# Last 128 output rows: from two halves copied by ScalarE and VectorE to three pieces copied by ScalarE alone

## The chip, the cores and the metric

The kernel runs on one core of a Trainium2 chip. The metric is the device time of one execution in microseconds, here the median over several runs. A core has engines with instruction queues of their own: TensorE (matmuls; its weight loads are listed apart), VectorE, ScalarE, GpSimd, and SyncE, which issues DMAs. ScalarE and GpSimd can issue DMAs too. TensorE writes its results to PSUM; VectorE and ScalarE copy them to SBUF, and a DMA carries them from there to HBM.

## The reference

A causal attention with a sliding window of 64, on 8 batches, 8 heads, 576 positions and 64 dimensions per head, followed by a gated feed-forward layer on the 4608 tokens of 512 values:

```
scores = scale * q @ k.T                 # per batch and head
mask   = (rel >= 0) & (rel < 64)         # rel = query position - key position
attn   = softmax(where(mask, scores, -1e9))
x      = (attn @ v)  as [4608, 512]      # heads side by side
out    = (maximum(x @ w_gate, 0) * (x @ w_val)) @ w_out    # d_ff = 1536
```

Inputs and output are float32; the output has 4608 rows of 512 columns.

## The kernel before

The tokens are cut into four tiles of 384 and six tiles of 512 (`starts`, `widths`). For each tile, attention makes `xt`, the transposed input of the feed-forward layer, in fp16. `hidden(t)` then multiplies it with slices of `w_gate` and `w_val` (L468), ScalarE takes the relu (L453), and VectorE multiplies both halves into `g_sb`, which holds the 12 slices (`NF`) of d_ff with the tile's tokens (L456). `output(t)` multiplies `g_sb` with `w_out`: for each block of 128 rows, 12 matmuls of 512 columns accumulate in one PSUM bank (L482, in `out_mm`), where the slice of `g_sb` is the stationary operand, so that each matmul has its own weight load of 128x128. `out_evac` copies the bank to SBUF on ScalarE (L489) and SyncE issues the store (L490).

The order is written by hand in a manual schedule: TensorE's feed-forward work is emitted in program order, and a planner (`Weaver`) with an estimated clock emits copies and the attention of the next tile at due times between the matmuls. At the end of the last tile its heap is empty (`W.drain()`), and everything comes out in program order.

The last tile ends in `output_last`. Its first three row blocks go through `output`. The last 128 rows are made in two halves of 256 columns, each with 12 matmuls (L514) into a PSUM tile of its own. The first half is copied by ScalarE and stored over SyncE's queue; the second half is copied in two quarters, one by ScalarE, stored over ScalarE's own queue, one by VectorE, stored over SyncE's queue (L520, L521).

Two rotations matter. The PSUM tiles come from `f_ps` (L84): four banks under one tag that `op_tile` and the `h` tiles of `hidden` share. The SBUF tiles `o_sb` come from `f_sb` (L83): three buffers, so that a fourth `o_sb` must wait until the store of the first has landed. The pool `consts` (L76) has one buffer for each name and is never rotated. At the end of the program (L699) the queues wait for all stores and for each other.

Of the kernel before, what the change touches and what calls it, by code (L numbers as in the profile page):

```python
# [10 lines left out]
FP32 = mybir.dt.float32  # L11
# [33 lines left out]
def kernel(  # L45
# [10 lines left out]
    nc = tc.nc  # L56
    B, H, S, D = q.shape
    DM = H * D
# [14 lines left out]
    starts = [TT * t for t in range(NS)] + [NS * TT + WT * t for t in range(NL)]  # L73
    widths = [TT] * NS + [WT] * NL

    consts = ctx.enter_context(tc.tile_pool(name="consts", bufs=1))  # L76
# [6 lines left out]
    f_sb = ctx.enter_context(tc.tile_pool(name="f_sb", bufs=3))  # L83
# [5 lines left out]
    wo = persist.tile([128, NF, DM], FP16)  # L89
# [403 lines left out]
    def op_tile():  # L493
        return f_ps.tile([128, DM], FP32, name="op", tag="h")

    def output(t, subs=None):
        for sub in range(widths[t] // 128) if subs is None else subs:
            op = op_tile()
            for f in range(NF):
                if f % 4 == 0:  # L500
                    W.advance(W.clock)
                out_mm(t, op, sub, f)
            out_evac(t, op, sub)

    def output_last(t):

        last = widths[t] // 128 - 1
        output(t, range(last))
        W.drain()
        for col in range(2):  # L510
            op = op_tile()
            for f in range(NF):
                g_sb, _ = gs[t]
                nc.tensor.matmul(op[:, 0:256], g_sb[:, f, bass.ds(last * 128, 128)], wo[:, f, 256 * col:256 * col + 256],  # L514
                                 start=(f == 0), stop=(f == NF - 1))
            parts = ((0, 256, nc.scalar.copy, nc.sync),) if col == 0 else (
                (0, 128, nc.scalar.copy, nc.scalar), (128, 256, nc.vector.tensor_copy, nc.sync))
            for c0, c1, copy, queue in parts:
                o_sb = f_sb.tile([128, DM], FP32, name="o_sb")
                copy(o_sb[:, c0:c1], op[:, c0:c1])  # L520
                queue.dma_start(out[bass.ds(starts[t] + last * 128, 128), 256 * col + c0:256 * col + c1], o_sb[:, c0:c1])  # L521

    def output_by_rows(t):
        ops = [op_tile() for _ in range(TT // 128)]
# [8 lines left out]
    with tc.manual_schedule():  # L533
# [134 lines left out]
        for t in range(2, NS + NL):  # L668
            ready(t)
            ahead(t)  # L670
            hidden(t, ((0, widths[t]),))
            (output if t < NS + NL - 1 else output_last)(t)
# [31 lines left out]
```

The softmax here doesn't subtract the row's maximum and nothing guards it: scores larger than these inputs give would overflow.

## Time and profile before

The median of four runs is 325.01 us (324.95 to 325.02).

| What | Value |
|---|---|
| time of the profiled execution | 325.0 us |
| its span | 323.3 us |
| mean granted TensorE clock | 0.989 |
| TensorE busy | 314.1 us, 97% |
| weight loads busy | 168.7 us |
| VectorE busy | 192.5 us, 60% |
| ScalarE busy | 127.0 us, 39% |
| GpSimd busy | 93.8 us, 29% |
| matmuls of 512 columns, L482 | 420, 93.9 us |
| matmuls of the last 128 rows, L514 | 24, 2.8 us |
| copies of whole row blocks, L489 | 35, 586 ns each |
| stores, 37 of L490 and L521 by SyncE, 1 by ScalarE | 256, 128 or 64 KB |

In the profile a line such as "L520 ACT COPY o_sb<-op" is read as: kernel line 520, on ScalarE (ACT), a copy from `op` to `o_sb`. PE is TensorE, PEld its weight loads, DVE VectorE, POOL GpSimd, SP SyncE; a "q" behind a name stands for the engine's instruction queue, where DMA issues and semaphore waits are shown. A timeline row gives start and duration in microseconds, merged over the "x" instructions that follow one another, and in brackets the idle time before the first and what ended it. In the list of stores, the last figure is the time from issue to landing in microseconds. The span starts with the first instruction.

### The profile page before, as it was taken

Reading aid. Unit: us, or ns where it says so; the run is one execution under the profiler, and the core shown is the slowest. Engines: PE = TensorE matmul, PEld = TensorE weight load, DVE = VectorE, ACT = ScalarE, POOL = GpSimd, SP = SyncE. Lnnn points to the kernel's source line nnn. Section 1 sums busy time; section 2 is a strip of 40 time slices with the busy share of each in tenths; the row PEclk is TensorE's granted clock in tenths of the full one; section 3 lists DMA queues with packets and bytes.
Section 4 is the critical chain, followed back from the end, with each engine's and each line's share of the span. In section 5 each row is a group of like instructions: output and inputs, shape, how many; then the busy total and the mean of one; then the engine's idle time right before and its main releaser. Section 6 shows DMA issues by size and latency. Waiting matters only on the chain.

```text
span 323.3 us, 8901 instructions
## 1 busy us (share of the span) xinstructions
PE 314.1 (97%) x3851; PEld 168.7 (52%) x3851; DVE 192.5 (60%) x370; ACT 127.0 (39%) x249; POOL 93.8 (29%) x138
## 2 busy tenths in 40 slices
PE   6699999999999999999999999999999999999995
PEld 2586958656556644454445444454445444544443
DVE  5947962687938749564755656674767146723410
ACT  3444324534424523532454234613372237223321
POOL 8766335285900390029000910081000000000000
PEclk9699999999999999999999999999999999999999
DMA  7999998979490179019900892091001200020002
GB/s 216 182 194 209 195 111 175 155 136 177 68 208 21 12 105 187 3 10 127 211 6 2 111 209 18 2 124 68 0 2 38 97 0 2 21 111 3 0 34 98
DMA packets 52488, 29.48 MB, mean 91 GB/s; under 512 B 38880, under 2 KB 43872, under 8 KB 52448
## 3 DMA queue, kind: packets, MB, share of 16 engines
q0 software_dynamic: 46688, 18.29, 48.3%
q1 hardware_dynamic: 5616, 10.55, 9.0%
q8 instruction: 30, 0.49, 0.6%
q14 instruction: 10, 0.08, 0.1%
q10 hardware_dynamic: 144, 0.07, 0.1%
HBM read 37.75 MB, written 9.44 MB: 146 GB/s over the span
## 4 chain that ended last, share of the span: by engine, by line
PE 94%; DVE 2%; DMA 2%; ACT 0%; issue 0%; DVEq 0%
PE h L468 59%; PE op L482 28%; PE st L233 3%; PE pv L371 2%; PE pv L293 2%; DMA k<-in_k_dram 1%; DVE kT L185 1%; DVE qT L185 1%; DMA out_dram<-o_sb 1%; ACT k L178 0%; DVE q L178 0%; ACT o_sb L489 0%; DVE v L200 0%; PE st L207 0%; DVE o_sb L520 0%
## 5 line engine op out<-in xcount | busy, mean ns | idle before, releaser
L456 DVE TENSOR_TENSOR g_sb<-r_sb,h 128x512 f16<-128x512 f32 (+1 forms) x120 | 75.4, 631 | 86.3 <-PE h L468 84.6
L468 PE MATMUL h<-xt,wg 128*128 128x512 f16 (+2 forms) x544 | 112.6, 338 | 0.1
L468 PE MATMUL h<-xt,wv 128*128 128x512 f16 (+2 forms) x544 | 111.3, 335 | 0.0
L453 ACT ACTIVATE r_sb<-h 128x512 f32<-128x512 f32 (+1 forms) x120 | 66.7, 558 | 89.5 <-PE h L468 82.7
L482 PE MATMUL op<-wo,g_sb 128*128 128x512 f16 x420 | 93.9, 379 | 0.0
L468 PEld LDWEIGHTS <-wg 128*128 128x128 f16 x544 | 51.7, 99 | 42.7 <-issue 0.5
L468 PEld LDWEIGHTS <-wv 128*128 128x128 f16 x544 | 50.5, 98 | 40.7
L482 PEld LDWEIGHTS <-g_sb 128*128 128x128 f16 x420 | 40.3, 98 | 47.2
L191 POOL DMA_DIRECT2D v<-in_v_dram x41 | 34.5, 857 | 94.7 <-PE pv L371 90.1
L489 ACT COPY o_sb<-op 128x512 f32<-128x512 f32 x35 | 20.5, 586 | 84.7 <-PE op L482 84.5
L356 DVE TENSOR_TENSOR pw<-pw,mask 128x512 f16<-128x512 f16 x48 | 19.3, 422 | 14.6 <-ACT pw L352 14.3
L352 ACT ACTIVATE pw<-st 128x512 f16<-128x512 f32 x48 | 25.7, 605 | 5.0 <-PE st L233 4.5
L200 POOL COPY v<-v 64x512 f16<-64x512 f16 (+1 forms) x21 | 15.5, 736 | 24.1 <-DMA v<-in_v_dram 23.3
L185 DVE STREAM_TRANSPOSE kT<-k 128x576 f32<-128x576 f32 x16 | 19.9, 1246 | 0.2 <-ACT k L178 0.2
L185 DVE STREAM_TRANSPOSE qT<-q 128x576 f32<-128x576 f32 x16 | 19.4, 1239 | 0.1
L267 ACT ACTIVATE p<-st 128x384 f16<-128x384 f32 (+1 forms) x40 | 14.0, 441 | 8.2 <-PE st L233 8.1
L391 DVE TENSOR_TENSOR xw<-pv,rw 128x448 f16<-128x448 f32 (+1 forms) x36 | 16.3, 507 | 0.4
L202 POOL COPY v<-v 64x512 f16<-64x512 f16 (+1 forms) x21 | 16.0, 762 | 1.0
L233 PEld LDWEIGHTS <-kT 32*128 32x128 f16 x1152 | 10.7, 94 | 10.3 <-issue 8.2
L233 PE MATMUL st<-qT,kT 32*128 32x64 f16 x1152 | 12.9, 192 | 3.3 <-DVE qT L185 3.3
L396 DVE STREAM_TRANSPOSE xt<-xw 128x1024 f16<-128x1024 f16 x12 | 14.9, 1245 | 0.4
L272 DVE TENSOR_TENSOR p<-p,mask 128x384 f16<-128x384 f16 x24 | 9.6, 419 | 3.4 <-ACT p L267 3.2
(46 smaller groups left out, 98.8 us busy)
## 6 DMA issues: line engine op xcount, KB each, us to landing
out_dram<-o_sb SPq DMA_DIRECT2D x35, 256.0 KB, 3.0
k<-in_k_dram POOLq DMA_DIRECT2D x15, 288.0 KB, 5.4
q<-in_q_dram POOLq DMA_DIRECT2D x15, 288.0 KB, 8.6
v<-in_v_dram POOLq DMA_DIRECT2D x31, 128.0 KB, 9.1
wg<-in_moe_w_gate_dram POOLq DMA_DIRECT2D x6, 256.0 KB, 6.5
wv<-in_moe_w_val_dram POOLq DMA_DIRECT2D x6, 256.0 KB, 8.3
wo<-in_moe_w_out_dram POOLq DMA_DIRECT2D x3, 512.0 KB, 12.2
v<-in_v_dram POOLq DMA_DIRECT2D x10, 64.0 KB, 5.9
```

The lines of the kernel that those rows point to most:

```text
L185: nc.vector.transpose(dst.rearrange("p (i j) -> p j i", i=32)[:, j0:j1], src[:, j0:j1])
L191: nc.gpsimd.dma_start(v16s[b % 2][lo:hi, g, :, 0:64], v[b, :, 64 * g - 64 + lo:64 * g - 64 + hi].rearrange("h p d -> p h d"))
L202: copy(t[0:64, g0:g1:2, h0:h1, 0:64], t[64:128, g0 - 1:g1 - 1:2, h0:h1, 0:64])
L233: return [lambda dh=dh: nc.tensor.matmul(to, kTs[b % 2][rows, hh, 64 * w:64 * w + 128, dh], qTs[b % 2][rows, hh, 64 * w:64 * w + 64, dh], ...
L352: nc.scalar.activation(d["p"][g].rearrange("p n c -> p (n c)"), d["st"][g], ACT.Exp, scale=scale)
L356: nc.vector.tensor_tensor(p, p, mask[:, None, :].to_broadcast([128, 2 * QW, 64]), MUL)
L391: nc.vector.tensor_tensor(d["x"][:, hh, s0:s1], pv[:, :, 0:D].rearrange("p s (c e) -> p s e c", e=2), d["r"][:, hh, s0:s1, :, None].to_bro ...
L453: nc.scalar.activation(part(r_sb), part(h1), ACT.Relu)
L456: nc.vector.tensor_tensor(g_sb[:, f:f + w, c0:c0 + n], part(r_sb), part(h2), MUL)
L468: nc.tensor.matmul(h[:, b * n:b * n + n], wt[:, c, (f + b) * 128:(f + b) * 128 + 128], xt[:, c, c0:c0 + n], start=(c == 0), stop=(c == NC ...
L482: nc.tensor.matmul(op, g_sb[:, f, bass.ds(sub * 128, 128)], wo[:, f], start=(f == 0), stop=(f == NF - 1))
L489: nc.scalar.copy(o_sb, op)
```

## The change

The last 128 rows are made in three pieces, of 256, 128 and 128 columns, each with 12 matmuls into a PSUM tile of its own. Each piece is copied whole by ScalarE into a tile of its own from `consts` (1 KB, 512 and 512 bytes in each partition). The first two stores go over SyncE's queue, the last over ScalarE's.

```
-        for col in range(2):
+        for c0, c1, queue in ((0, 256, nc.sync), (256, 384, nc.sync), (384, DM, nc.scalar)):
             op = op_tile()
             for f in range(NF):
                 g_sb, _ = gs[t]
-                nc.tensor.matmul(op[:, 0:256], g_sb[:, f, bass.ds(last * 128, 128)], wo[:, f, 256 * col:256 * col + 256],
+                nc.tensor.matmul(op[:, 0:c1 - c0], g_sb[:, f, bass.ds(last * 128, 128)], wo[:, f, c0:c1],
                                  start=(f == 0), stop=(f == NF - 1))
-            parts = ((0, 256, nc.scalar.copy, nc.sync),) if col == 0 else (
-                (0, 128, nc.scalar.copy, nc.scalar), (128, 256, nc.vector.tensor_copy, nc.sync))
-            for c0, c1, copy, queue in parts:
-                o_sb = f_sb.tile([128, DM], FP32, name="o_sb")
-                copy(o_sb[:, c0:c1], op[:, c0:c1])
-                queue.dma_start(out[bass.ds(starts[t] + last * 128, 128), 256 * col + c0:256 * col + c1], o_sb[:, c0:c1])
+            o_sb = consts.tile([128, c1 - c0], FP32, name=f"o_last{c0}")
+            nc.scalar.copy(o_sb, op[:, 0:c1 - c0])
+            queue.dma_start(out[bass.ds(starts[t] + last * 128, 128), c0:c1], o_sb)
```

## The prediction

> **What bounds the kernel now.** I read the page's busy shares first, then the chain that ended last, then the last six microseconds in order of time, then single lines.
>
> ```profile
> PE 314.1 (97%) x3851; PEld 168.7 (52%) x3851; DVE 192.5 (60%) x370; ACT 127.0 (39%) x249; POOL 93.8 (29%) x138
> ...
> PE 94%; DVE 2%; DMA 2%; ACT 0%; issue 0%; DVEq 0%
> ```
>
> TensorE is busy for 97% of the span and 94% of the chain. Nothing ahead of the last 128 rows is in the diff, so up to the start of their matmuls (317.12 us) the instruction streams are the same; what can change is the tail, 317.1 to 323.3 us, where the chain leaves TensorE:
>
> ```profile
> 317.32 0.59 ACT o_sb L489
> 317.92 0.02 issue
> 317.94 2.00 DMA out_dram<-o_sb
> 319.94 0.03 issue
> 319.97 0.05 DVEq L520
> ...
> 320.31 0.04 issue
> 320.35 0.29 DVE o_sb L520
> ```
>
> The chain does not go through the last matmuls at all. It goes from the copy of the row block before (L489) through the landing of its store at 319.94, then four semaphore instructions on VectorE's queue, then VectorE's copy. That is a buffer being waited for: `o_sb` has three buffers, and VectorE's is the fourth tile from that row block's, so it takes the same buffer and must wait for its store. In order of time:
>
> ```profile
> 317.12 2.78 PE L514 MATMUL op<-wo,g_sb 128*128 128x256 f16 x24
> 318.68 0.37 ACT L520 COPY o_sb<-op 128x256 f32<-128x256 f32 x1 [0.77 <-PE op L514]
> 319.99 0.27 ACT L520 COPY o_sb<-op 128x128 f32<-128x128 f32 x1 [0.94 <-PE op L514]
> 320.28 0.37 ACTq L521 DMA_DIRECT2D out_dram<-o_sb  x1
> 320.35 0.29 DVE L520 COPY o_sb<-op 128x128 f32<-128x128 f32 x1 [10.04 <-ACT o_sb L520]
> ...
> 320.67 0.33 SPq L521 DMA_DIRECT2D out_dram<-o_sb  x1
> ```
>
> TensorE ends at 317.12 + 2.78 = 319.90. ScalarE starts its half at 319.99, VectorE its half only at 320.35. (The releaser named there, ScalarE's copy, is the last event in time by coincidence: the four waits run one after another at 97 ns each from 319.97.) So SP issues the last store at 320.67, 0.39 us after ScalarE's.
>
> ```profile
> out_dram<-o_sb ACTq DMA_DIRECT2D x1, 64.0 KB, 1.6
> out_dram<-o_sb SPq DMA_DIRECT2D x1, 64.0 KB, 1.7
> ```
>
> SP's store lands at 320.67 + 1.7 = 322.37, ScalarE's at about 321.9; SP's closing waits (L699) pass at 321.9 and 322.4, in agreement. The span ends at 323.3, 0.93 us after the last landing. The profiled execution took 325.00 us, 1.7 more than its span; the median of the runs shown is 325.01, so I subtract straight from 325.0.
>
> **The change part by part.**
>
> *Removed: VectorE's copy, its four waits, and SP's last store behind it.* With three tiles of their own nobody waits for the row block's store. What ends last is then ScalarE's third copy and the store that ScalarE issues.
>
> *Added: twelve matmuls.* The second half was 12 matmuls of 256 columns; it becomes 24 of 128, each with its own load of 128x128 weights (g is the stationary operand, so loads go from 24 to 36). This lies wholly on the path, and no matmul of 128 moving columns with a full weight load is in the trace. The start-to-start pitch from the rows: at 256 columns (2.78 - 0.272)/23 = 109.1 ns; the others are
>
> ```profile
> 18.52 2.80 PE L468 MATMUL h<-xt,wv 128*128 128x192 f16 x32
> ...
> 309.35 7.93 PE L482 MATMUL op<-wo,g_sb 128*128 128x512 f16 x36
> ...
> 103.10 0.68 PE L233 MATMUL st<-qT,kT 32*128 32x64 f16 x64
> 103.10 0.57 PEld L233 LDWEIGHTS <-kT 32*128 32x128 f16 x64 [0.32 <-issue]
> ```
>
> At 192 columns (2.80 - 0.246)/31 = 82.4 ns, at 512 (7.93 - 0.379)/35 = 215.7. All three are columns/2.4 ns plus 2.4, so in all of them the streaming sets the pitch and the weight load is hidden. On that line 128 columns take 55.7 ns: the low end, since the columns must stream. The high end from the rows is 82.4, the shortest pitch at which a full weight load is seen hidden. The score matmuls (L233) say more: 64 loads, each a quarter of the array's rows and all 128 columns, come every (0.57 - 0.094)/63 = 7.6 ns, so each row group gets new weights of 128 columns every 30 ns. If a full load does its four row groups as these do, it hides below 55.7 ns. The 98 ns that the profile gives one load is latency, as loads of 98 ns stand 82 ns apart in the 192-column stretch. I take 55.7.
>
> Here the Trainium skill speaks against the change. "TensorE: Matmul & The Clock Gate", section "Back-to-back issue gap", gives about 81 ns for each load-and-matmul pair at 128 columns against 56 for the matmul alone, and 131 at 512. This trace has 215.7 at 512, with a load for each, so the pair figures do not hold here and the formula (columns/2.4 + 2.5) does. That section's 81 would be close to my high end; its neighbour "LDWEIGHTS (loading the stationary operand)", 128 columns/1.2 = 107 ns, would be worse, and is refuted as a serial cost by 82.4.
>
> Then the end of TensorE. The first piece's 12 matmuls take 12 x 109.1 = 1.309 us, so the second piece starts at 318.43. 23 pitches of 55.7 are 1.281; the last matmul's own duration falls on the line 379, 326, 272, 246 (for 512, 384, 256, 192 columns) to 219 ns. End: 318.43 + 1.28 + 0.22 = 319.93, **0.03 later** than now. By 81 it would be 320.51, by 82.4 320.54, by 107 321.11.
>
> *Added: a third PSUM tile.* Four banks rotate; the third piece takes the bank of the row block two before, emptied at 314.73 + 0.59 = 315.32, nearly 4 us early. Costs nothing; its cover would have to slip by that much.
>
> *ScalarE's copies.* Three rather than two, in program order on ScalarE: 0.37, 0.27, 0.27. The second starts at about 319.3 and is over by 319.6, ahead of the third's matmuls (319.93), so it hides; if TensorE were more than twice as fast here it would not. The copies start 0.09 after their matmuls now, where those of L489 start 0.04 after. The difference fits ScalarE's queue: ahead of each L520 copy stands a separate semaphore wait (1307 and 1246 ns, until the matmuls end), with a second wait for the old buffer in the copy. With new tiles one wait is left: between 0 and -0.05; I take -0.05, the L489 row.
>
> *Stores.* SP: first piece at about 319.05 (issue 0.33 us), second at about 319.6, free by then; 128 and 64 KB, landed by 321.3 at 1.7 each. ScalarE's queue holds its store behind its copy, as now, and nothing behind it. All 16 DMA engines are idle when it starts. The skill's "DMA: Bandwidth & Descriptors", section "Issuing engines are not separate DMA queues", says that another issuing engine saves only issue time. The rows agree (1.6 against 1.7 us to landing): the queue is worth 0 to 0.1 us, as SP would be free too; the gain is the wait.
>
> *2 KB more of SBUF per partition* shifts the tiles placed behind it: no row prices that, I take 0, with a few tenths either way in the range.
>
> **Sum.** Third copy starts 319.93 + 0.04 = 319.97, ends 320.24; issue at 320.26 (now 320.28 for the same queue); landing + 1.6 = 321.86, against 322.37: 0.51 earlier. With 0.09 before the copy, 0.46. I take 0.5: span 322.8, **time 324.5 us**, -0.15%. A measurement of this kernel tells about 0.2%, 0.65 us, from no change, so I forecast a real but hardly measurable gain.
>
> **The rivals.**
>
> *Weight loads set the pitch* (81 to 82.4 ns). For: the skill's figure, and nothing in the trace shows a full load under 82. Against: L233's 30 ns. TensorE ends at 320.54, landing 320.54 + 0.33 + 1.6 = 322.47: 0.1 later than now, 325.1 us. Break-even is a pitch of 78 ns.
>
> *Slower: loads not overlapped with one another at all*, one at a time at 107 ns, in pieces of 128 columns on L514: TensorE ends at 321.11, landing 323.04, +0.67, 325.7 us. It decides, beyond 0.2%, from a pitch of 106 ns. Against it: 82.4 ns with the same load.
>
> *The change does not shorten the end*: the last store lands later than its 1.6, say the 2.0 us of the row block's store (256 KB, so too high for 64 KB). Gain 0.1, 324.9 us. For it: ScalarE's queue carries just one store, so 1.6 is one sample. Against: SP's 64 KB needs 1.7.
>
> *A shift elsewhere*, by addresses or by the phase of the instruction fetches: more than 0.65 us either way, 323.8 or 325.7. For: 2 KB moved. Against: runs within 0.07 us and an unchanged stream ahead.
>
> **How the numbers follow.** Forecast 0.72 (own range 324.25 to 324.75), loads at about 82 ns 0.10, serial loads 0.03, late landing 0.09, shift elsewhere 0.06. The range from 324.2 to 325.2 takes in the first, second and fourth and leaves out serial loads and shifts, plus some of the forecast's tail. Faster by over 0.2% (below 324.36): about a seventh of the forecast's cases and half of the shifts, 0.14. Slower (above 325.66): half of the shifts and part of the serial loads, 0.05. Within: 0.81.
>
> **What would show it.** The last two pieces' 24 matmuls in about 1.28 + 0.22 = 1.50 us (rival: 2.1, 2.7); no VectorE instruction after 310.3; ScalarE's third copy at 319.97 and its store issued at 320.26; span end about 0.93 after a landing at 321.9. Wrong if the 128-column pitch is over 78 ns, if that store takes 2 us to land, or if the matmuls of the last rows do not start at 317.1.

## The result: 0.1% faster, and where the profile after shows it

The changed kernel takes 324.77 us (median), the kernel before 325.10 in the same measurement: a ratio of 0.9990, 95% interval 0.9986 to 0.9995, or 0.33 us less (0.16 to 0.45). That is inside 0.2% and inside the forecast range, with two thirds of the forecast gain of 0.5. It lies just outside the forecast's own narrower range of 324.25 to 324.75; the kernel before was 0.09 us longer in this measurement than in the one the forecast started from.

The profiled execution of the changed kernel does not show this at first sight: its span is 323.5 us, longer than the 323.3 of before.

```profile
span 323.5 us, 8919 instructions
...
PE 314.8 (97%) x3863; PEld 169.3 (52%) x3863; DVE 192.0 (59%) x369; ACT 127.3 (39%) x250; POOL 94.0 (29%) x138
```

The cause lies at the beginning of the kernel. In the table of stretches, the one from 14.7 to 19.7 us has a mean granted TensorE clock (the figure after the count of matmuls) of 0.78 before and 0.64 after: in this execution the full clock was granted later. First before, then after:

```profile
14.70:19.70 5.00, 5.00 (x47) 0.78 1.23 201
```

```profile
14.70:19.70 5.00, 4.97 (x40) 0.64 1.23 202
```

The 192-column matmuls with `w_val` start at 19.11 in place of 18.52, and the last 128 rows at 317.71 in place of 317.12: 0.59 us late in both places. So from here on each run is measured from the start of its first L514 matmul to the end of its span, which I call the **tail**. The views give spans and landings to 0.1 us; with the trace's own times it is 323.268 - 317.123 = 6.145 us before and 323.488 - 317.714 = 5.774 after, 0.37 less. That agrees with the times. (The expectations below start from the rounded spans, 6.18 and 5.79.)

The tail of the changed kernel in order of time, and its last store's time to landing (the L514 row carries the shape of its first matmuls; 24 of the 36 have 128 columns):

```profile
317.71 2.81 PE L514 MATMUL op<-wo,g_sb 128*128 128x256 f16 x36
317.92 0.59 ACT L489 COPY o_sb<-op 128x512 f32<-128x512 f32 x1 [2.00 <-PE op L482]
319.23 0.37 ACT L517 COPY o_last<-op 128x256 f32<-128x256 f32 x1 [0.72 <-PE op L514]
319.62 0.90 SPq L518 DMA_DIRECT2D out_dram<-o_last  x2
319.89 0.27 ACT L517 COPY o_last<-op 128x128 f32<-128x128 f32 x1 [0.30 <-PE op L514]
320.56 0.27 ACT L517 COPY o_last<-op 128x128 f32<-128x128 f32 x1 [0.40 <-PE op L514]
320.86 0.37 ACTq L518 DMA_DIRECT2D out_dram<-o_last  x1
...
out_dram<-o_last ACTq DMA_DIRECT2D x1, 64.0 KB, 1.7
```

36 matmuls take 2.81 us where 24 took 2.78. The third copy starts 0.04 us after TensorE ends, the last store is issued 3.15 us into the tail (before: 320.67 - 317.12 = 3.55) and lands 1.7 later. The chain that ended last now runs straight through TensorE; the store's landing and the semaphores on VectorE's queue are gone from it:

```profile
310.11 7.77 PE op L482 x36
317.88 2.67 PE op L514 x36
320.54 0.02 issue
320.56 0.27 ACT o_last L517
```

### The profile page after: what moved, and what is told of

Read it like the earlier page. It is cut to its first block, busy times and chain, and to the rows that moved or that the text cites. A ratio compares the mean times of both kernels' runs of the same rounds, so it can differ in the third digit from the quotient of the medians.

```text
span 323.5 us, 8919 instructions
## 1 busy us (share of the span) xinstructions
PE 314.8 (97%) x3863; PEld 169.3 (52%) x3863; DVE 192.0 (59%) x369; ACT 127.3 (39%) x250; POOL 94.0 (29%) x138
## 4 chain that ended last, share of the span: by engine, by line
PE 95%; POOL 2%; DMA 2%; issue 0%; ACT 0%; POOLq 0%
PE h L468 59%; PE op L482 28%; PE st L233 3%; PE pv L371 2%; DMA v<-in_v_dram 2%; PE pv L293 1%; PE op L514 1%; POOL v L191 1%; POOL k L167 0%; POOL v L202 0%; POOL v L200 0%; POOL q L167 0%; PE st L207 0%; POOL ident L107 0%; POOL ident L111 0%
## 5 line engine op out<-in xcount | busy, mean ns | idle before, releaser
L489 ACT COPY o_sb<-op 128x512 f32<-128x512 f32 x35 | 20.5, 586 | 84.7 <-PE op L482 84.5
```

The costliest lines, as they stand in the source:

```text
L489: nc.scalar.copy(o_sb, op)
```

## The experiments

The change did three things together: it took away the wait for a rotated SBUF buffer, it took away a PSUM tile read by two engines, and it moved the last copy to ScalarE. The first four runs take these apart, the next four try other pieces and the other queue, and the last four follow up a surprise. Times into the tail, in us, from the trace's own times of one profiled execution for each kernel; "landed" is the last landing of all stores, "after landing" the rest of the tail. Transfers are those over SP's and ScalarE's queues in the whole kernel. Two tails can be compared only as far as one execution goes, and most of the times differ from before by no more than their interval; what an engine waits for is read from the rows.

| kernel | transfers | last store issued | landed | tail | after landing | ratio to before (95%) |
|---|---|---|---|---|---|---|
| before | 40 | 3.55 | 5.22 | 6.15 | 0.92 | |
| changed | 40 | 3.15 | 4.86 | 5.77 | 0.92 | 0.9990 (0.9986 to 0.9995) |
| own SBUF tiles alone | 40 | 3.44 | 5.10 | 6.02 | 0.92 | 1.0001 (0.9993 to 1.0009) |
| own PSUM tiles alone | 40 | 3.54 | 5.20 | 6.11 | 0.92 | 0.9996 (0.9988 to 1.0004) |
| both, third copy by VectorE | 40 | 3.17 | 4.83 | 5.74 | 0.91 | 0.9989 (0.9981 to 0.9997) |
| changed, rotating SBUF tiles | 40 | 3.21 | 4.93 | 5.85 | 0.92 | 0.9991 (0.9983 to 0.9999) |
| changed, last store over SP | 40 | 3.14 | 4.80 | 5.73 | 0.93 | 0.9985 (0.9978 to 0.9991) |
| two halves of 256 | 39 | 3.22 | 5.00 | 6.51 | 1.50 | 1.0004 (0.9996 to 1.0012) |
| 256, 128, 64, 64 | 41 | 3.12 | 4.65 | 6.44 | 1.79 | 1.0005 (0.9996 to 1.0014) |
| 384, 128 | 39 | 3.12 | 4.86 | 6.36 | 1.51 | 1.0000 (0.9992 to 1.0009) |
| 384, 128, one early store in two | 40 | 3.11 | 4.86 | 5.97 | 1.11 | 0.9998 (0.9990 to 1.0006) |
| changed, one early store in two | 41 | 3.14 | 4.76 | 6.58 | 1.82 | 1.0014 (1.0008 to 1.0021) |
| changed, eight early stores in two | 48 | 3.15 | 4.92 | 5.84 | 0.92 | 0.9994 (0.9980 to 1.0009) |
| 256, 128, 64, 64, seven early stores in two | 48 | 3.30 | 5.53 | 6.51 | 0.98 | 1.0007 (0.9999 to 1.0015) |

### Tiles of their own alone

Edit, on the kernel before:

```
-                o_sb = f_sb.tile([128, DM], FP32, name="o_sb")
-                copy(o_sb[:, c0:c1], op[:, c0:c1])
-                queue.dma_start(out[bass.ds(starts[t] + last * 128, 128), 256 * col + c0:256 * col + c1], o_sb[:, c0:c1])
+                o_sb = consts.tile([128, c1 - c0], FP32, name=f"o_last{256 * col + c0}")
+                copy(o_sb, op[:, c0:c1])
+                queue.dma_start(out[bass.ds(starts[t] + last * 128, 128), 256 * col + c0:256 * col + c1], o_sb)
```

> The kernel before, with the three SBUF tiles of the last 128 rows taken from consts, one each, and nothing else changed: two halves, the second half's PSUM tile still read by ScalarE and VectorE. I measure the tail, from the start of the first L514 matmul to the end of the span: 6.18 us before, 5.79 after. Buffer theory (the prediction's: VectorE's copy starts late because its buffer waits for the row block's store and four semaphore instructions): VectorE starts 0.04 us after TensorE ends, 2.82 us into the tail, and the tail is about 5.8; time -0.35 us. Bank theory (VectorE's copy waits for ScalarE's copy of the other half of the same PSUM tile, and the buffer's wait lies beside that): ScalarE's quarter runs from 2.82 to 3.09, VectorE starts at about 3.14 in place of 3.23, and the tail is 6.1; time -0.1 us.

The prediction's reading falls. With no buffer to wait for, VectorE still starts late. The chain that ended last in this run:

```profile
317.36 2.63 PE op L514 x24
320.00 0.02 issue
320.02 0.27 ACT o_last L520
320.29 0.02 issue
320.31 0.29 DVE o_last L520
```

VectorE follows 0.02 us after ScalarE's copy of the other quarter. The compiled program says why. In it the waits of VectorE's copy, in the kernel before and in this one, are

```
before:    L520 TensorCopy o_sb<-op   128x128 [waits DMAHW4, DMAHW3, DMAHW5, DMAHW2, DMAHW6, DMAHW1, DMAHW7, DMAHW0, Activation]
own tiles: L520 TensorCopy o_last<-op 128x128 [waits Activation]
```

The eight DMAHW are the semaphores of the stores (the buffer's wait). The last wait is on ScalarE, for its read of the same PSUM tile, and it stays; the trace agrees, for in this run the copy waits for one semaphore alone, the one that ScalarE's copies raise. The start moves from 3.23 to 3.11 us into the tail and the tail by 0.12; the time shows no gain (1.0001, at best 0.9993).

### PSUM tiles of their own alone

Edit, on the changed kernel: `o_sb = f_sb.tile([128, DM], FP32, name="o_sb")` again, third piece copied by `nc.vector.tensor_copy` and stored over SP, second stored over ScalarE's queue.

> The split alone: three pieces of 256, 128 and 128 columns, each in a PSUM tile of its own, but with the rotating o_sb tiles of before; ScalarE copies the first two, VectorE the third; stores over SP, ScalarE's queue, SP. Nobody shares a PSUM tile; the buffer's wait on the row block's store stays. Buffer theory: VectorE starts 3.23 to 3.3 us into the tail as before, tail 6.2, time 0. Bank theory, if the buffer's wait costs nothing of its own: VectorE starts at about 2.9, tail 5.85, time -0.3 us. If both waits end at about the same time (each hides the other), this run is at 6.2 and the one with tiles of its own at 6.1.

Here nobody shares a PSUM tile, and the buffer's wait is what is left, at the same place. The chain:

```profile
317.96 2.00 DMA out_dram<-o_sb
319.96 0.03 issue
319.99 0.05 DVEq L517
...
320.33 0.04 issue
320.37 0.29 DVE o_sb L517
```

VectorE starts 320.37 - 317.15 = 3.22 us into the tail, as before. So the two waits of the kernel before ended within about 0.1 us of one another, and each hid the other: this is the third outcome in the expectation. It rests on the rows: the time's interval (0.9988 to 1.0004) takes in both no gain and the changed kernel's.

### Both, with VectorE's copy kept

Edit, on the changed kernel: third piece copied by `nc.vector.tensor_copy`, stored over SP; second piece stored over ScalarE's queue.

> The changed kernel with the third piece copied by VectorE and stored over SP, the second stored over ScalarE's queue: a PSUM tile and an SBUF tile of its own for each piece. Both theories: VectorE starts 2.85 us into the tail (TensorE's end 2.81 + 0.04), copies for 0.29, SP issues at 3.17, landing at 4.85, tail 5.8, within 0.05 of the changed kernel: then it is the two waits and not the engine that counted. If VectorE as such is slower here (a third theory), the tail stays over 6.0.

```profile
317.38 2.81 PE L514 MATMUL op<-wo,g_sb 128*128 128x256 f16 x36
...
320.23 0.29 DVE L517 COPY o_last<-op 128x128 f32<-128x128 f32 x1 [9.66 <-PE op L514]
```

VectorE starts 2.85 us into the tail, 0.04 after TensorE, and the time is the changed kernel's (0.9989 against 0.9990). With both waits gone it does not matter which engine copies last.

### Rotating tiles, with ScalarE copying

Edit, on the changed kernel: `o_sb = f_sb.tile([128, DM], FP32, name="o_sb")` for the three tiles.

> The changed kernel with its three tiles taken from the rotating o_sb buffers again: ScalarE's third copy takes the buffer of the row block before, whose store lands 2.82 us into the tail, where TensorE ends at 2.81. ScalarE has one semaphore to wait for there, not eight. Both theories: third copy at 2.86 to 2.95, tail 5.8 to 5.9, time -0.3 us against before. If the buffer is dear whoever waits for it, the third copy starts at 3.2 and the tail is 6.15.

```profile
320.13 0.01 issue
320.15 0.04 ACTq L517
320.19 0.04 issue
320.23 0.27 ACT o_sb L517
```

The same buffer's wait costs ScalarE 0.08 us (320.23 - 320.15), tail 5.85. VectorE had four semaphore instructions, 0.38 us from 319.99 to the copy's start at 320.37 in the run with own PSUM tiles alone, because it had to wait for all eight of the stores' semaphores; ScalarE's third copy waits for one of them. So it was not the landing that made the buffer dear, but the instructions that waited for it. The tiles of their own are worth 0.08 us of tail here.

### The last store over SP

Edit, on the changed kernel: `(384, DM, nc.sync)`.

> The changed kernel with its last store over SP's queue in place of ScalarE's. SP has issued the second piece's store long before. If the queue is worth only issue time: issue at 3.15 us into the tail in both, landing 1.6 to 1.7 later, tail 5.75 to 5.85 (5.79 in the changed kernel), time -0.3 us against before. If ScalarE's queue as such is quicker or slower, the tail differs by over 0.1.

Tail 5.73, 0.05 below the changed kernel's; 1.66 us to landing against 1.71. ScalarE's queue brings nothing. The time of 0.9985 against 0.9990 is the lowest ratio of all, with intervals that overlap.

### Other pieces, and a surprise

Edits, on the changed kernel, of the list of pieces alone:

```
two halves:  ((0, 256, nc.sync), (256, DM, nc.scalar))
384:         ((0, 384, nc.sync), (384, DM, nc.scalar))
64:          ((0, 256, nc.sync), (256, 384, nc.sync), (384, 448, nc.sync), (448, DM, nc.scalar))
```

> The changed kernel in two pieces of 256 columns, each copied whole by ScalarE into a tile of its own, the second stored over ScalarE's queue: no wait on a buffer or on another reader, and no further matmuls. TensorE ends at 2.78 us into the tail, the copy of 256 columns takes 0.37 from 2.82, issue at 3.22, landing of 128 KB at 4.9, tail 5.85; time -0.3 us against before. If it is the third piece that brought the gain, the tail is 6.1 or more.

> The changed kernel with the last 128 columns in two pieces of 64, 12 more matmuls and weight loads; the first of them is stored over SP, the second over ScalarE's queue. This asks where full weight loads begin to set the pitch. Streaming alone would be 64/2.4 + 2.4 = 29 ns: TensorE ends 2.84 us into the tail, tail 5.7. Loads that bind at one column per cycle of the 2.4 GHz clock, 53 ns: the last 24 matmuls take 0.6 us more, TensorE ends at 3.4, tail 6.25. Loads that bind at 82 ns: TensorE ends at 4.05, tail 6.9; but 82 is out since the 128-column matmuls ran at 55.7.

> The changed kernel in two pieces of 384 and 128 columns, both copied by ScalarE, stored over SP and ScalarE's queue: 12 matmuls and loads fewer than in the changed kernel. On the line of the pitches 12 x 162.4 + 11 x 55.7 + 219 ns: TensorE ends at 2.78 in place of 2.81. ScalarE's copy of 384 columns (about 0.48 us from 2.15) is over at 2.63, before the second piece's end, so the last copy is not held up: 2.82 to 3.09, issue at 3.12, landing at 4.8, tail 5.75. If the larger first store is in the way of the last one, the tail is over 5.85.

Up to the issue of the last store all three went as expected: 3.22, 3.12 and 3.12 us into the tail. The run with 64 settles the pitch:

```profile
317.77 2.84 PE L514 MATMUL op<-wo,g_sb 128*128 128x256 f16 x48
```

Take away 12 x 109.1 and 12 x 55.7 ns for the first two pieces and 193 for the last matmul's own duration: (2840 - 1309 - 668 - 193)/23 = 29 ns. That is the 29 ns of the prediction's line, 64/2.4 + 2.4, so a full weight load of 128x128 every 29 ns stays hidden and the streaming of 64 columns is still the limit.

But all three tails are over 6.3, and none is faster than the kernel before. The loss comes after the landing: 1.5 and 1.8 us to the end of the span, not 0.9. In all three the number of transfers is no longer 40. At the end of the program SP walks nine semaphore instructions, its closing waits, then runs two DRAIN instructions, and then all engines meet. Here they are for the run with 384 and 128, by stretches (321.0 to 322.2, and 322.5 to 322.8; there is no SP instruction between 322.2 and 322.5):

```profile
L696 SPq EVENT_SEMAPHORE  x3: 28/28/28, 321.7 to 322.1; - x3
...
L696 SPq DRAIN  x2: 7/68/130, 322.6 to 322.8; - x2
```

Both stores have landed by 322.0, yet SP stands still for some 0.4 us before it drains. In the kernel before and in the changed kernel nothing of the kind follows the landing. The changed kernel, 320.5 to 321.0, 321.0 to 321.4, 321.4 to 322.2, 322.2 to 322.62 and after that:

```profile
L696 SPq EVENT_SEMAPHORE  x6: 28/28/28, 320.6 to 320.9; - x6
...
L696 SPq EVENT_SEMAPHORE  x1: 28/28/28, 321.3 to 321.3; - x1
...
L696 SPq EVENT_SEMAPHORE  x1: 28/28/28, 321.8 to 321.8; - x1
...
L696 SPq EVENT_SEMAPHORE  x1: 28/28/28, 322.6 to 322.6; - x1
...
L696 SPq DRAIN  x2: 7/7/7, 322.7 to 322.7; - x2
```

Six go through early; the last three wait for the three stores in turn, and the last store is the last of them. With 40 transfers the two halves would stand at 5.00 + 0.92 = 5.92, an estimate from the table that no run tested: between before and changed, so that part of the gain is the smaller last piece.

### Only the number of transfers

Edit, in `out_evac`, for the first row block of the fifth token tile, whose stores are issued at 146 us; the last 128 rows of the kernel that it is applied to are left as they are:

```
-            nc.sync.dma_start(out[bass.ds(starts[t] + sub * 128, 128)], o_sb)
+            cuts = (0, 256, DM) if t == 4 and sub == 0 else (0, DM)
+            for c0, c1 in zip(cuts, cuts[1:]):
+                nc.sync.dma_start(out[bass.ds(starts[t] + sub * 128, 128), c0:c1], o_sb[:, c0:c1])
```

First it is applied to the changed kernel:

> The changed kernel, its last 128 rows untouched, with the same early row block stored in two halves: 41 transfers in place of 40. Closing theory: the last store moves on to the first of the eight semaphores that SP waits for, the other waits and the idle 0.4 us come after its landing (as in the run with pieces of 64, which had 41): tail 6.5 to 6.8 in place of 5.79, time +0.4 us against before. Piece theory: tail 5.8, time -0.3 us as the changed kernel.

This shows it: the last copy and the last store are where they were in the changed kernel (issue at 3.14, landed at 4.76), and the kernel is 0.14% slower than before, with the changed kernel 0.10% faster. In the first line below SP goes past one semaphore and then waits for the last store, in the second five follow that landing at 322.0, then comes the idle stretch (322.34 to 322.7, no instruction), and in the third the other three:

```profile
L698 SPq EVENT_SEMAPHORE  x1: 28/28/28, 320.1 to 320.1; - x1
...
L698 SPq EVENT_SEMAPHORE  x5: 28/28/28, 322.0 to 322.3; - x5
...
L698 SPq EVENT_SEMAPHORE  x3: 27/28/28, 322.8 to 322.9; - x3
```

The transfers take eight semaphores in turn, and SP waits for these in one order, so the 41st transfer stands near its beginning where the 40th stands at its end. (In the traces the last store raises semaphore 117 with 39 transfers, 118 with 40 and 108 with 41; the closing waits reach 108 second, 117 eighth and 118 ninth.) Eight instructions 60 to 95 ns apart and 0.4 us of idling, which lay beside the landing, come after it.

Then to the kernel with 384 and 128:

> Two pieces of 384 and 128 columns as before, and one early row block (the first of the fifth token tile, 100 us and more before the end) stored in two halves of 256 columns, so that the kernel has 40 transfers over SP's and ScalarE's queues again, as the kernel before and the changed one have. The run with 39 had its last copy and store where they were expected (issue 3.11 us into the tail) and still a tail of 6.33: 1.5 us from the landing to the end of the span, 0.93 in the others; SP issued nothing for 0.4 us after its last wait. Closing theory (SP's closing waits walk the stores' eight semaphores in a fixed order, and where the last store stands in it, which the count of transfers sets, decides whether SP's idle 0.4 us is hidden behind the landing): tail 5.75, time -0.35 us against before. Piece theory (a piece of 384 columns, or two stores at the end, as such are slow): tail 6.3 again, time +0.1.

About two thirds of it: the tail goes from 6.36 to 5.97, not to 5.75. The last store is now the last to be waited for, but the idle stretch has moved too. SP passes its last but one semaphore at 321.77 and the last at 322.21, though that store landed at 322.06:

```profile
L698 SPq EVENT_SEMAPHORE  x1: 28/28/28, 321.8 to 321.8; - x1
...
L698 SPq EVENT_SEMAPHORE  x1: 28/28/28, 322.2 to 322.2; - x1
```

Next, eight early row blocks in the changed kernel (`t in (4, 5) and sub < 4` in the first line of the edit):

> The changed kernel with eight early row blocks (fifth and sixth token tiles) stored in two halves each: 48 transfers, so that the rotation over eight semaphores ends where it does with 40, while SP's instruction stream is longer by eight issues and their waits. If the order of the closing waits alone decides: tail 5.8 as in the changed kernel. If SP's idle 0.4 us stands at a fixed place of its instruction stream (its instructions being fetched, say) and that place counts: tail 5.8 if the place now falls before the closing waits or among those that wait anyway, 6.2 if it falls after the landing. A shorter store of 128 KB costs nothing there.

Tail 5.84, 0.06 more than with 40. The idle stretch has left the closing waits. It is ahead of the second piece's store now, which SP issues 0.80 us after the first where it was 0.57 in the changed kernel, though ScalarE's copy was over at 319.72:

```profile
319.18 1.13 SPq L520 DMA_DIRECT2D out_dram<-o_last  x2
```

Over these runs it moves forward as SP's stream grows: after the ninth closing instruction with 38 issues on SP, after the eighth with 39 (the run with 384), after the sixth or fifth with 40, before the last rows' second store with 47. Counted over all of SP's recorded instructions it is one place: in all 14 traces 0.41 to 0.47 us pass between the end of the 79th and the start of the 80th. In four of them (before, changed, own SBUF tiles alone, rotating) a store that SP waits for there lands at the end of that time and would hide a stall; in the other ten, at 0.41 to 0.42 us, none does. That is a stall at a fixed place of SP's instruction stream. Its cause stays open. In every trace the one 8 KB packet of the tail on the DMA queue for instructions starts 1.04 to 1.36 us after that 79th instruction; it moves with the stall, but it begins when the stall is already over, so it is not what SP waited for.

Last, seven early row blocks (`4 * t + sub in range(16, 23)`) in the kernel with pieces of 256, 128, 64 and 64:

> The kernel with pieces of 256, 128, 64 and 64 columns, and seven early row blocks (fifth and sixth token tiles) stored in two halves each: 48 transfers, so that the last store stands last among the closing waits and SP's idle 0.4 us falls before them, as in the changed kernel with 48. The last copy and store were timed with 41: issue 3.12 us into the tail, landing 1.5 later. Closing theory: landing at 4.62, end of the span 0.95 later, tail 5.55 to 5.65 (5.79 in the changed kernel, 6.43 with 41), time -0.55 us against before, which would be the shortest of all. If a tail of four stores as such is slow, it stays over 6.0.

A miss. The closing waits were in order (0.98 us after the landing), but the stores were not: SP issued the third piece's store 0.83 us after the second's (1.16 - 0.33), and both stores of 32 KB took 2.2 us to land, 1.6 and 1.5 in the run with 41:

```profile
319.51 1.16 SPq L520 DMA_DIRECT2D out_dram<-o_last  x2
```

The late issue is the stall at its new place. Why the landings were slow stays open. The same sign is in the run before this one: SP's store of 64 KB took 2.0 us there and 1.6 in the changed kernel. These two runs are the only ones of the 14 in which that 8 KB packet of instructions runs while the data of the last stores is being written; that it slowed them was not tested.

## Why the prediction was right, and where it was wrong

**The added matmuls: right.** The 128-column pitch was put at 55.7 ns and TensorE's end at 0.03 later. The matmuls took 2.81 us against 2.78, their starts 55 to 56 ns apart at 128 columns, which refutes both rivals on weight loads (81 to 82.4, and 107 ns); 29 ns at 64 columns says it again. The 81 ns for a load-and-matmul pair, which the prediction quotes from the Trainium skill's "TensorE: Matmul & The Clock Gate", section "Back-to-back issue gap", was the wrong guide here; the trace's 215.7 ns at 512 columns had said so.

**The copy and the issue: right.** The third copy starts 0.04 after TensorE, as the L489 row had it; issue was forecast 320.26 - 317.12 = 3.14 into the tail and came at 3.15.

**The landing: mis-sized by 0.1.** The term was 1.6, the one sample of ScalarE's queue; it measured 1.71, and the old last store's 1.7 was 1.67. These two are most of the way from the forecast 0.51 to the 0.37 of the tails. It is a mild form of the rival with the late landing. Why it took 1.71 stays open: in the run with 41 transfers the same store took 1.62.

**The cause of VectorE's late start: wrong.** The step said that the buffer's wait held VectorE, and that ScalarE's copy as releaser was a coincidence. It was a wait in its own right: without the buffer's wait VectorE started 0.02 us after ScalarE. The chain of before went through the buffer because that wait ended last, by little. "The gain is the wait" should have been "the gain is both waits": with either one left VectorE starts at 3.11 and 3.22 us into the tail, with both gone at 2.85, and the times are 1.0001 and 0.9996 against 0.9989. The sum came out because the change happens to remove both: that part was luck.

**A term that the sum did not have.** The 0.93 us after the landing was carried over as a constant. It held (0.92 in both), for the changed kernel has 40 transfers like the one before; that too was luck. With 39 or 41 it is 1.5 to 1.8, and the increase is more than the whole gain.

**Shift elsewhere.** Nothing in the tail needs it. One of the prediction's signs of being wrong did turn up, for the matmuls of the last rows started at 317.71 and not at 317.1. That is the profiled execution's own shift of 0.59, which came with the later clock: in the 14 profiles these matmuls start anywhere between 317.04 and 318.40. Not all of that is the clock: the latest, the run with the last store over SP, is 0.17 us behind the profile of before at `w_val` and 1.27 at the last rows. The times of both kernels spread by over a microsecond (324.52 to 325.82, and 324.51 to 326.22 before); what else is in that spread was not followed.

## What to carry to other kernels

When a row names one releaser and the chain goes through another wait, both can be real: remove one in the mind and ask when the other ends, before you credit the whole gap to either. Two engines that read one PSUM tile were put one behind the other here by the compiled waits, so a split between engines wants a PSUM tile for each. At the end of a program, look at the closing waits as well as at the last store: an edit of the tail that changes the number of transfers can lose there what it won.

## What the runs showed of the hardware that was not expected

- Full weight loads of 128x128 hide behind matmuls of 64 columns, at 29 ns from start to start.
- An engine that waits for eight store semaphores pays four semaphore instructions, 97 ns each (VectorE), where ScalarE with one paid 0.08 us.
- SP's closing instructions come 60 to 95 ns apart, and there is a stall of 0.41 to 0.42 us between the 79th and the 80th of its recorded instructions. One early store in two, at 146 us, took the changed kernel's tail from 5.77 to 6.58 us and its time from 0.9990 to 1.0014 of before.
- From the last landing to the end of the span it was 0.91 to 0.93 us wherever the last store is the last to be waited for and the stall lies elsewhere (eight runs), and up to 1.82 where it is not.
- One execution's span can hide a gain of 0.4 us in a tail: the granted clock of the stretch from 14.7 to 19.7 us was 0.78 in one profile and 0.64 in the other.
